# Batches 1 and 2: the next batch's first hash in one piece behind the first gate and value pair, instead of in two pieces around it

## The chip, the cores and the metric

The kernel runs on one core of one Trainium2 chip. The metric is the device time of one execution in microseconds (us); a lower one is better. A version is told by the median of several runs, and a separate execution is profiled.

## The reference

Four batches of eight heads, 768 positions and a head size of 64. Attention is masked by a hash: query and key see each other only where the signs of six projections agree. The attended heads, side by side, are the 512 wide input `x` of a gated layer with a residual.

```
q_bits = (einsum('bhsd,dk->bhsk', q, proj) > 0)        # 6 bits, the same for k
mask   = q_bucket[:, :, :, None] == k_bucket[:, :, None, :]
scores = where(mask, (q @ k.T) / sqrt(64), -1e9)
attn   = softmax(scores);  x = attn @ v                # heads side by side: 3072 x 512
h      = gelu(x @ w_gate) * (x @ w_val)                # 3072 x 1536
out    = x + sigmoid(x @ w_res) * (h @ w_out)
```

## The kernel before, in words

**The stages.** Work goes batch by batch. The attention of a batch takes 36 slots (four pairs of heads, nine chunks each): `scores` (L373) multiplies keys and queries into a PSUM tile `sp` and ScalarE takes the exponential to `e` (L385), and `values` (L345) multiplies `e` by the values into `av`, two slots later. `finish` (L299) divides on VectorE (L306, L307) and, for the batches in the middle, has SyncE issue a DMA transpose of the result `x_tok` to `x_sb` (L310), one per pair of heads. Then comes the gated layer's first half, `gate_val` (L403): for each of twelve blocks `m`, TensorE multiplies `x_sb` by `wg` into one `sp` tile (the gate) and by `wv` into the other (the value), L399, with four steps of the contraction each; one step is a matmul of 512 columns and one of 256. ScalarE takes the gelu of the gate (L416) and VectorE multiplies it by the value into `hh` (L419). There are only two `sp` tiles, so that the next block's gate waits for the gelu of this one's, and the next block's value for the product of this one's.

The layer's second half, `project` (L425), is a generator that hands out one matmul at a time: for each of six row tiles four matmuls with `wr` into `rps` (L431, ScalarE takes its tanh, L435) and twelve with `wo` into `fps` (L445), then two VectorE operations (L448, L451) and a store from SyncE (L453). The matmuls of batch b's projection are spread over the attention slots of batch b+1, some are kept (`HELD`), and `mlp_mm(NMM)` issues all that are left.

**The hash.** The raw queries and keys of a pair are transposed in blocks of 32 on VectorE (`tr`, L194, to `t32`). `hash_mm` (L197) multiplies them by the projection in float32: four operands (the two pairs' queries and keys) stand in the four column strips of the array, 32 columns each, beside one another, and write one PSUM tile `hs`. `hashed(ps, i0, i1)` (L515) issues steps i0 to i1 of four steps; a step is four matmul instructions of the program, which the profile shows as eight matmuls. So the whole hash of two pairs is x32 in the profile and half of it x16, all at L205. Then `tokens` transposes `hs` back (L215, VectorE), `bits` compares with zero and writes the bits beside the cast data in `nat` (L224, VectorE), and `turn` has SyncE issue a DMA transpose of `nat` to `aug` (L248), which the next batch's `scores` read.

**The order.** It is written out by hand: the program's order is each engine's order, and the pools only add the waits. At the end of the attention of batch 1 and of batch 2 the program issues, on TensorE: three of the four contraction steps of gate and value for m = 0 (`begun`, the last step needs the last pair's `x_sb`), what is left of the projection, the first half of the hash of the next batch's first two pairs, and then `gate_val`, which issues the last step of gate and value for m = 0 (four matmuls), calls `beside()` (the second half of the hash), and goes on with m = 1 to 11. Behind m = 0 the list `gv_work` (L585) puts `tokens` of that hash. Batch 0 and batch 3 have orders of their own, which the change leaves as they are. A second hash, of the other two pairs, stands whole behind block m = 6 (L592).

Of the kernel before, what the change touches and what calls it, by code (L numbers as in the profile page):

```python
# [17 lines left out]
def kernel(  # L18
# [178 lines left out]
    def hash_mm(jobs, dhs=(0, 1), hs_=(0, 1)):  # L197
        if jobs[0] not in hsum:
            hsum[jobs[0]] = mm_ps.tile([P, HT, 32], FP32, tag="r", name="hs")
        hs = hsum[jobs[0]]  # L200
        for hh in hs_:
            sl = slice(hh * T, hh * T + T)
            for dh in dhs:
                for j, x in enumerate(jobs):
                    nc.tensor.matmul(hs[32 * j:32 * j + 32, sl], projw[:, dh, :],  # L205
                                     t32[x][:, sl, dh, :], start=(dh == 0), stop=(dh == 1),
                                     tile_position=(0, 32 * j))
# [127 lines left out]
    def x_turn(b, hp):  # L335
        pt = mm_ps.tile([P, T, P], BF16, tag="f" if b == 0 else "r", name="pt")
        for t in range(T):
            nc.tensor.transpose(pt[:, t, :], x_tok[b][:, hp, t, :], ident)
        if hp == HP - 1:
            nc.scalar.activation(x_sb[b][:, hp, 0:2], pt[:, 0:2], AF.Copy)  # L340
            nc.vector.tensor_copy(x_sb[b][:, hp, 2:T], pt[:, 2:T])
        else:
            nc.vector.tensor_copy(x_sb[b][:, hp], pt)

    def values(p, c, e):  # L345
        va = vaug[p]
        for i in range(2):
            hi, parts = banks[2 * c + i]
            first = p < HP and (p, hi) not in av
            opened(p, hi)  # L350
            off = i * 512
            for (jt, qt0, nq) in parts:
                for qt in range(qt0, qt0 + nq):
                    nc.tensor.matmul(av[p, hi][:, qt, :], e[:, off:off + P],  # L354
                                     va[:, hi, jt, 0:D + 1],
                                     start=first, stop=(p >= HP and jt == T - 1),
                                     skip_group_check=True)
                    first = False
                    off += P
            if (2 * c + i + 1) % NCH == 0:  # L360
                if p < HP:
                    preset(p, hi)
                if (p, hi) not in late:
                    finish(p, hi)
# [4 lines left out]
    def flush():  # L369
        while pending:  # L370
            values(*pending.pop(0))

    def scores(p, c):  # L373
        qs, ks = aug[p, 0], aug[p, 1]
        sp = sc_ps.tile([P, 1024], FP32, tag="sp", name="sp")
        for i in range(2):
            hi, parts = banks[2 * c + i]
            off = i * 512
            for (jt, qt0, nq) in parts:
                nc.tensor.matmul(sp[:, off:off + nq * P], ks[0:KA, hi * T + jt, :],  # L380
                                 qs[0:KA, hi * T + qt0:hi * T + qt0 + nq, :],
                                 start=True, stop=True)
                off += nq * P
        e = e_pool.tile([P, 1024], BF16, tag="e", name="e")
        nc.scalar.activation(e, sp, AF.Exp, scale=float(ALPHA))  # L385
        return p, c, e
# [6 lines left out]
    def gv_mm(b, m, w, k0, k1, sp=None):  # L393
        xs = x_sb[b].rearrange("p k t n -> p k (t n)")
        if sp is None:
            sp = sc_ps.tile([P, 1024], FP32, tag="sp", name="sp")
        for kk in range(k0, k1):
            for c0, c1 in ((0, 512), (512, S)):
                nc.tensor.matmul(sp[:, c0:c1], w[:, kk, bass.ts(m, P)], xs[:, kk, c0:c1],  # L399
                                 start=(kk == 0), stop=(kk == KM - 1))  # L400
        return sp

    def gate_val(b, begun, beside):  # L403
        for m in range(KF):
            ps = []
            for i, w in enumerate((wg, wv)):
                if m == 0:
                    sp = gv_mm(b, m, w, KM - 1, KM, begun[i])
                else:
                    sp = gv_mm(b, m, w, 0, KM)  # L410
                ps.append(sp)
                if m == 0 and i == 1:
                    beside()
                if w is wg:
                    gt = g_pool.tile([P, S], BF16, tag="gt", name="gt")
                    nc.scalar.activation(gt, sp[:, 0:S], AF.Gelu)  # L416
            if m == 0:
                hidden[b] = hh_pool.tile([P, KF, S], BF16, tag="hh", name="hh")
            nc.vector.tensor_mul(hidden[b][:, m, :], gt, ps[1][:, 0:S])  # L419
            for piece in gv_work.pop((b, m), []):  # L420
                piece()
# [78 lines left out]
    def gv(b, m, *pieces):  # L500
        gv_work.setdefault((b, m), []).extend(pieces)
# [13 lines left out]
    def hashed(ps, i0=0, i1=4):  # L515
        jobs = [(p, side) for p in ps for side in range(2)]
        for i in range(i0, i1):
            hash_mm(jobs, (i % 2,), (i // 2,))
# [84 lines left out]
    def mlp_mm(n):  # L603
        while mlp and n > 0:
            try:
                next(mlp[0])
                n -= 1
                done[0] += 1
            except StopIteration:
                mlp.pop(0)  # L610

    for s in range(LAST):
        p, c = divmod(s, NCH)
        b, slot = divmod(s, NSLOT)
        cur = scores(p, c)
        for piece in side_pe.pop(s, []):
            piece()
        if b >= 1:
            mlp_mm(AHEAD + (slot + 1) * (NMM - HELD - AHEAD) // NSLOT - done[0])
        pending.append(cur)  # L620
        while len(pending) > LAG:
            values(*pending.pop(0))
        for piece in side_work.pop(s, []):
            piece()
        if slot == NSLOT - 1:
            values(*pending.pop(0))
            ps = (HP * (b + 1), HP * (b + 1) + 1)
            if b == 0:
                nc.scalar.activation(table, warm[:, 0:1], AF.Gelu)
                begun = [gv_mm(0, 0, wg, 0, KM - 1)]  # L630
                values(*pending.pop(0))
                begun.append(gv_mm(0, 0, wv, 0, KM - 1))
                x_turn(b, HP - 1)
                hashed(ps, 0, 3)
                gate_val(b, begun, lambda: hashed(ps, 3, 4))
            else:
                mlp_mm(4)
                flush()
                begun = [gv_mm(b, 0, w, 0, KM - 1) for w in (wg, wv)]
                if b < B - 1:  # L640
                    mlp_mm(NMM)
                    hashed(ps, 0, 2)
                    gate_val(b, begun, lambda: hashed(ps, 2, 4))
                else:
                    x_turn(b, HP - 1)
                    mlp_mm(HELD - 7)
                    gv(b, 0, lambda: mlp_mm(NMM))
                    gate_val(b, begun, lambda: mlp_mm(3))
            done[0] = 0
            mlp.append(project(b))  # L650
# [33 lines left out]
```

## Time and profile before

| | |
|---|---|
| median of three runs | 347.27 us (346.83 to 347.31) |
| profiled execution, from its first to its last instruction (span) | 345.9 us, 1.4 below that median |
| TensorE matmuls (PE) busy | 337.9 us, 98% of the span |
| VectorE (DVE), ScalarE (ACT), GpSimd (POOL) busy | 191.5, 206.9 and 86.1 us |
| granted TensorE clock, mean | 1.000 |
| hash matmuls of L205 | 3% of the chain that ended last |

Of the profiled execution no other time than its span is known; what lies around the span, the start and the end of the program, is taken as the 1.4 us between span and median. The chain that ended last is followed back from the last instruction, at each step to what released it or to the instruction before it on its engine. A piece of it gives the start and the length in us, the engine, the tile and the line, and how many instructions it holds.

### The profile page before, as it was taken

How to read it: one execution, taken by the hardware profiler on the slowest of the kernel's cores; microseconds unless marked ns; L12 is line 12 of the kernel's file. 1: busy time of each engine (PE TensorE's matmuls, PEld its weight loads, DVE VectorE, ACT ScalarE, POOL GpSimd, SP SyncE). 2: the span in 40 equal slices, each digit the busy share in tenths (PEclk: the TensorE clock that was granted, in tenths of full speed). 3: DMA queues.
4: the chain of work that ended last, by engine and by line, in shares of the span. 5: the costliest groups of instructions: out<-in, count | busy, mean ns of one | idle time of the engine just before them, and what ended most of it. 6: DMA issues, size and time to landing. Idle time of an engine off the chain costs nothing.

```text
span 345.9 us, 7597 instructions
## 1 busy us (share of the span) xinstructions
PE 337.9 (98%) x3112; PEld 204.4 (59%) x3112; DVE 191.5 (55%) x403; ACT 206.9 (60%) x232; POOL 86.1 (25%) x162
## 2 busy tenths in 40 slices
PE   8999999999999999999999999999999999999994
PEld 5667665655666655555666665655566665556442
DVE  6877757755344856757344784747244444333333
ACT  3889973226999952225999882222999984223120
POOL 4779940343055000270044100242030000000000
PEclk9999999999999999999999999999999999999999
DMA  7939999979376843518366642725430220000022
GB/s 218 377 67 239 247 265 195 159 89 223 121 178 196 195 106 78 106 34 154 85 182 190 223 117 61 136 48 105 79 100 32 55 55 30 32 1 0 32 75 78
DMA packets 71171, 42.90 MB, mean 124 GB/s; under 512 B 49504, under 2 KB 68192, under 8 KB 71136
## 3 DMA queue, kind: packets, MB, share of 16 engines
q1 hardware_dynamic: 64720, 37.17, 42.4%
q0 software_dynamic: 6336, 5.24, 10.2%
q8 instruction: 24, 0.39, 0.4%
q14 instruction: 11, 0.09, 0.1%
q10 hardware_dynamic: 80, 0.00, 0.0%
HBM read 29.36 MB, written 6.29 MB: 103 GB/s over the span
## 4 chain that ended last, share of the span: by engine, by line
PE 89%; ACT 5%; DVE 3%; issue 1%; DMA 1%; SPq 0%; DVEq 0%; ACTq 0%
PE sp L399 36%; PE fps L445 18%; PE sp L380 15%; PE av L354 8%; PE rps L431 5%; ACT e L385 4%; PE hs L205 3%; PE pt L259 2%; DMA ld<-in_q_dram 1%; DVE o L451 1%; DVE o L448 1%; DVE nat L224 0%; PE hs L234 0%; DVE ht L215 0%; DVE hh L419 0%
## 5 line engine op out<-in xcount | busy, mean ns | idle before, releaser
L385 ACT ACTIVATE e<-sp 128x1024 bf16<-128x1024 f32 x144 | 143.8, 1027 | 13.4 <-PE sp L380 7.8
L416 ACT ACTIVATE gt<-sp 128x768 bf16<-128x768 f32 x48 | 38.9, 811 | 93.0 <-PE sp L399 93.0
L380 PE MATMUL sp<-aug,aug 71*128 71x256 bf16 (+1 forms) x384 | 86.1, 325 | 1.1 <-ACT e L385 0.6
L445 PE MATMUL fps<-wo,hh 128*128 128x512 bf16 (+2 forms) x300 | 79.5, 370 | 0.0
L419 DVE TENSOR_TENSOR hh<-gt,sp 128x768 bf16<-128x768 bf16 x48 | 45.8, 955 | 50.5 <-PE sp L399 45.3
L399 PE MATMUL sp<-x_sb,wg 128*128 128x512 bf16 (+1 forms) x384 | 71.0, 326 | 0.1
L399 PE MATMUL sp<-x_sb,wv 128*128 128x512 bf16 (+1 forms) x384 | 70.9, 326 | 0.2 <-DVE hh L419 0.2
L354 PEld LDWEIGHTS <-e 128*128 128x128 bf16 x1152 | 53.3, 97 | 29.1 <-issue 1.4
L354 PE MATMUL av<-va,e 128*128 128x65 bf16 x1152 | 58.9, 193 | 0.1
L399 PEld LDWEIGHTS <-wv 128*128 128x128 bf16 x384 | 37.5, 98 | 25.1 <-issue 0.4
L399 PEld LDWEIGHTS <-wg 128*128 128x128 bf16 x384 | 36.6, 98 | 26.3 <-issue 3.0
L445 PEld LDWEIGHTS <-hh 128*128 128x128 bf16 x300 | 27.5, 97 | 22.7 <-issue 0.3
L448 DVE SCALAR_TENSOR_TENSOR o<-th,fps 128x512 f32<-128x512 f32 (+2 forms) x25 | 16.6, 666 | 36.6 <-PE fps L445 32.0
L380 PEld LDWEIGHTS <-aug 71*128 71x128 bf16 x384 | 29.4, 97 | 10.9 <-issue 2.1
L184 POOL TENSOR_SCALAR nat<-ld 128x768 bf16<-128x768 f32 (+1 forms) x16 | 14.1, 884 | 76.8 <-DMA aug<-nat 73.0
L281 POOL TENSOR_TENSOR v<-ldv 128x384 f32<-128x384 f32 x16 | 16.0, 998 | 66.7 <-DMA ldv<-in_v_dram 66.6
L194 DVE STREAM_TRANSPOSE t<-ld 128x768 f32<-128x768 f32 (+1 forms) x34 | 30.8, 913 | 1.2 <-DMA ld<-in_q_dram 1.0
L333 DVE COPY av<-av 128x390 f32<-128x390 f32 x24 | 13.6, 567 | 30.0 <-PE av L329 30.0
L431 PE MATMUL rps<-wr,x_sb 128*128 128x512 bf16 x96 | 27.1, 378 | 0.0
L435 ACT ACTIVATE th<-rps 128x512 f32<-128x512 f32 x24 | 14.3, 594 | 18.4 <-PE rps L431 18.4
L224 DVE TENSOR_SCALAR nat<-htp 32x72 bf16<-32x72 f32 x96 | 21.9, 228 | 1.8
L451 DVE SCALAR_TENSOR_TENSOR o<-o,x_tok 128x512 f32<-128x512 f32 (+2 forms) x25 | 18.2, 727 | 0.9
(61 smaller groups left out, 191.2 us busy)
## 6 DMA issues: line engine op xcount, KB each, us to landing
ldv<-in_v_dram SPq DMA_DIRECT2D x16, 384.0 KB, 5.5
out_dram<-o SPq DMA_DIRECT2D x23, 256.0 KB, 2.0
ld<-in_q_dram SPq DMA_DIRECT2D x15, 384.0 KB, 5.2
ld<-in_k_dram SPq DMA_DIRECT2D x15, 384.0 KB, 6.2
wg<-in_moe_w_gate_dram POOLq DMA_DIRECT2D x4, 384.0 KB, 8.0
wv<-in_moe_w_val_dram POOLq DMA_DIRECT2D x4, 384.0 KB, 9.8
wo<-in_moe_w_out_dram POOLq DMA_DIRECT2D x3, 512.0 KB, 6.2
wr<-in_moe_w_res_dram POOLq DMA_DIRECT2D x1, 512.0 KB, 12.8
```

Of the source, the lines that this page charges most:

```text
L194: nc.vector.transpose(t32[p, side][:, sl].rearrange("p c h n -> p (c h n)"), raw[p, side][:, sl].rearrange("p c d -> p (c d)"))
L224: engs[a % len(engs)].tensor_scalar(nat_of(x)[32 * a:32 * a + 32, :, D:D + NBITS], ht[32 * j:32 * j + 32, :, NBITS * a:NBITS * (a + 1)], 0 ...
L354: nc.tensor.matmul(av[p, hi][:, qt, :], e[:, off:off + P], va[:, hi, jt, 0:D + 1], start=first, stop=(p >= HP and jt == T - 1), skip_group ...
L380: nc.tensor.matmul(sp[:, off:off + nq * P], ks[0:KA, hi * T + jt, :], qs[0:KA, hi * T + qt0:hi * T + qt0 + nq, :], start=True, stop=True)
L385: nc.scalar.activation(e, sp, AF.Exp, scale=float(ALPHA))
L399: nc.tensor.matmul(sp[:, c0:c1], w[:, kk, bass.ts(m, P)], xs[:, kk, c0:c1], start=(kk == 0), stop=(kk == KM - 1))
L416: nc.scalar.activation(gt, sp[:, 0:S], AF.Gelu)
L419: nc.vector.tensor_mul(hidden[b][:, m, :], gt, ps[1][:, 0:S])
L431: nc.tensor.matmul(rps, x_sb[b][:, kk, t, :], wr[:, kk, :], start=(kk == 0), stop=(kk == KM - 1))
L445: nc.tensor.matmul(fps[:, cs], hh[:, m, bass.ts(t, P)], wo[:, m, cs], start=(m == 0), stop=(m == KF - 1))
L448: nc.vector.scalar_tensor_tensor(o[:, cs], th[:, cs], 1.0, fps[:, cs], op0=ALU.add, op1=ALU.mult)
L451: nc.vector.scalar_tensor_tensor(o3, o3, 0.5, x_tok[b][:, k0:k1, t, :], op0=ALU.mult, op1=ALU.add)
```

## The change

```diff
@@ -639,8 +639,7 @@
                 begun = [gv_mm(b, 0, w, 0, KM - 1) for w in (wg, wv)]
                 if b < B - 1:
                     mlp_mm(NMM)
-                    hashed(ps, 0, 2)
-                    gate_val(b, begun, lambda: hashed(ps, 2, 4))
+                    gate_val(b, begun, lambda: hashed(ps))
                 else:
                     x_turn(b, HP - 1)
                     mlp_mm(HELD - 7)
```

The branch is taken for b = 1 and b = 2. The hash's first two steps no longer stand between the rest of the projection and the last step of gate and value for m = 0; all four steps stand together behind that last step, and ahead of the gate of m = 1. No instruction is added or removed, and the order on VectorE, ScalarE, GpSimd and SyncE is the same as before.

## The prediction

> **What bounds the kernel now.** I read the page first: its busy times and its clock row.
>
> ```profile
> PE 337.9 (98%) x3112; PEld 204.4 (59%) x3112; DVE 191.5 (55%) x403; ACT 206.9 (60%) x232; POOL 86.1 (25%) x162
> ...
> PEclk9999999999999999999999999999999999999999
> ```
>
> TensorE is busy in 98% of the span, at the full granted clock in every slice, and no other engine is over 60%. In such a kernel what counts is how many nanoseconds TensorE's own stream takes, and whether a wait opens in it. Second, then, the chain that ended last, in order of time, around the place of the change in batch 1 (start us, length us, what):
>
> ```profile
> 127.65 2.59 PE fps L445 x12
> 130.24 0.79 PE hs L205 x16
> 131.03 0.76 PE sp L399 x4
> 131.78 0.79 PE hs L205 x16
> 132.57 15.71 PE sp L399 x96
> 148.28 1.44 PE hs L205 x32
> ```
>
> Here are the rest of the projection, the first half of the hash, the last contraction step of gate and value for m = 0, the second half, and then m = 1 to 6. The last row is the other hash, which stands whole. Every piece is TensorE's and each starts where the one before ends: nothing is waited for. Batch 2 shows the same lengths, from 210.73 (0.79, then 0.76, then 0.79) to 213.06. Third, what could come too late after the move: the timelines of SyncE, ScalarE and VectorE in the same stretch (start, length, engine, line, and in brackets the idle time before), and the landing time in the answer for the tile `x_sb`, from 120 to 134 us.
>
> ```profile
> 126.55 1.22 SPq L310 DMA_TRANSPOSE x_sb<-x_tok  x1
> ```
>
> ```profile
> 131.50 0.81 ACT L416 ACTIVATE gt<-sp 128x768 bf16<-128x768 f32 x1 [4.10 <-PE sp L399]
> ```
>
> ```profile
> 130.33 0.69 DVE L448 SCALAR_TENSOR_TENSOR o<-th,fps 128x512 f32<-128x512 f32 x1 [3.81 <-PE fps L445]
> 131.06 0.69 DVE L451 SCALAR_TENSOR_TENSOR o<-o,x_tok 128x512 f32<-128x512 f32 x1
> 132.34 0.95 DVE L419 TENSOR_TENSOR hh<-gt,sp 128x768 bf16<-128x768 bf16 x1 [0.59 <-ACT gt L416]
> 133.21 0.59 DVE L215 STREAM_TRANSPOSE htp<-hs 128x384 f32<-128x384 f32 x1
> ```
>
> ```profile
> DMA to landing us min/median/max: 2.7/2.7/2.7
> ```
>
> The reader is to see the release times: the last pair's `x_sb` has landed at 126.55 + 2.7 = 129.25, the gelu of m = 0 ends at 132.31, its product at 133.29.
>
> **The change part by part.** *TensorE's stream.* Nothing is added or removed; only the order differs, and with it how often TensorE goes from the whole array in bf16 to four strips in float32 and back: twice each way before, once after. The cost of that is in the rows. Two halves take 0.79 each, 1.58 together; the same 32 instructions in one piece take 1.44 (row at 148.28). That saves 0.14. The four gate and value matmuls take 0.76 between two hash halves; in the long row 96 of them take 15.71, so 0.164 each and 0.65 for four, when bf16 matmuls of the same array stand around them. Before them will then stand the projection's matmuls, also bf16 over the whole array; where these two kinds meet today the chain shows no charge (twelve of L399 from 125.70 take 1.95, 0.163 each, and twelve of L445 behind them 2.59, which ends where the next piece starts). The way into the hash stays and is inside the 1.44. So this saves 0.11. From 130.24 to the gate of m = 1 the path is now 132.57 - 130.24 = 2.33, and after 0.65 + 1.44 = 2.09: **0.24 us less, in each of two batches, 0.48 in all.** The bounds from both sides: the whole hash can't cost more here than two halves (then 0.11 per batch, 0.22 in all), unless something is waited for, which is a rival below; and no more than 0.24 can go, because all other instructions remain.
>
> *The wait for `x_sb`.* The last step of gate and value waits for the last pair's transpose. It moves from 131.03 to 130.24, and the transpose landed at 129.25: 0.99 to spare. Behind this wait stands all of TensorE. I cost it at nothing; the twelve projection matmuls (2.59) cover it. Without the cover it costs what the landing lies behind 130.24.
>
> *The wait for the gelu.* The gate of m = 1 needs the first `sp` tile. The gelu starts 131.50 - 131.03 = 0.47 after the gate's piece does and takes 0.81, so 1.28 in all. Before, 0.76 + 0.79 = 1.55 stood over it (0.27 to spare); after, 2.09 (0.81 to spare). Nothing, and safer than now.
>
> *VectorE.* Gelu is over at 130.24 + 1.28 = 131.52, but VectorE has L451 until 131.75. The product then runs from 131.75 to 132.70 and not from 132.34 to 133.29: 0.6 earlier. The value of m = 1 needs it at 132.33 + 1.31 = 133.64 (eight matmuls of 0.164 for the gate before it), so 0.9 is to spare. L215 comes next in VectorE's order and needs the whole hash, which ends at 132.33 instead of 132.57, so it starts no later than about 132.7 and not at 133.21. The four `bits` operations and the DMA transpose of L248 on SyncE follow, about half a microsecond earlier. TensorE waits for none of them in this stage: the `aug` that they make is read by the scores from about 163 on. So this is worth nothing; a later transpose would cost nothing either.
>
> *Behind this place.* From the gate of m = 1 on, all engines take their pace from TensorE. In batch 2's attention TensorE is busy for 39.82 of 40 us:
>
> ```profile
> 165.00:205.00 40.00, 39.82 (x454) 24.79 (x453) 22.56 (x44) 37.09 (x40) 9.42 (x16) 1.00 0.56 163
> ```
>
> (The first number after the length is TensorE's.) An earlier start is thus handed on almost whole. Loads are issued by slots in the program's order and move along.
>
> **Sum:** the profiled span of 345.9 becomes 345.4. What lies around it, 1.4, stays, so from the median of 347.27 comes 346.8, a gain of 0.14%. A measurement of this kernel can tell about 0.2% (0.7 us) from no change, so the likeliest verdict is no difference.
>
> **The rivals.** *First: the transpose is late, and the kernel gets slower.* Place: the first matmul of the last gate step in batches 1 and 2. Before, the first half of the hash stood ahead of this wait as work that didn't need `x_sb`. After, it stands behind. If the landing comes at a time X after 131.03, the old order ends at X + 0.76 + 0.79 and the new one at X + 0.65 + 1.44: 0.54 worse in each batch, 1.08 in both, 348.35 us. It decides from a landing of 130.24 + 0.24 = 130.48, that is 3.9 us after the issue instead of 2.7. For it: the thirteen transposes of L310 need 2.7 at least, 2.8 in the median and 6.6 at most, so longer ones occur. Against it: both that matter (126.55 and 207.04) landed after 2.7, and from 129.3 to 130.3 the DMA engines carry nothing. I give it 0.11. On this the Trainium skill speaks against the change: "DMA: Bandwidth & Descriptors", Rules for kernel authors, says to issue a DMA early and to wait on its semaphore late, with computation between. By that rule the hash belongs ahead of the wait; so far the trace says that the projection is computation enough.
>
> *Second: the gain is not handed on,* 347.27 (347.0 to 347.5). A transfer with a clock of its own would have to bound a later stage, or a new stall to take the 0.48 back. Against it are the 39.82 of 40 us; for it, that in this attention VectorE's L448 and L451 appear in the chain (178.68 and 179.40), so the cover there is thin. That the order is not changed as said belongs here; TensorE's instructions in the two programs show exactly this one move, twice. Together 0.12.
>
> *Third: more than the sum.* Near 177 and 187 VectorE's L451 takes 1.30 and 1.34 beside a busy GpSimd, against 0.69 at 131.06, and TensorE shows gaps there:
>
> ```profile
> 176.60:181.30 4.70, 4.64 (x52) 2.76 (x49) 2.56 (x4) 4.10 (x5) 3.85 (x7) 1.00 0.54 130
> 187.10:190.30 3.20, 3.09 (x32) 1.77 (x30) 2.14 (x3) 2.81 (x4) 3.04 (x7) 1.00 0.33 61
> ```
>
> Gaps of 0.06 and 0.11 could close if the stage falls differently: 0.17 in each of two later attentions, 0.34 in all, and 346.45 us. Nothing in the change moves GpSimd against VectorE there, so 0.10.
>
> **How the numbers follow.** The forecast has a chance of 0.67, at 346.8, and with the spread of the runs shown (0.48 from lowest to highest) its own range is 346.5 to 347.1. The range of 346.4 to 347.4 takes in the second and the third rival and leaves out the first, and the outer parts of the others. Faster by over 0.2% means under 346.58: most of the third rival (0.09) and the lower tail of the forecast (0.11), 0.20. Slower by over 0.2% means over 347.96: the first rival (0.11) and a stall of the second kind (0.02), 0.13. Within: 0.67.
>
> **What would show it.** In the chain after, around 130 us: L445, then four of L399 in 0.65, then 32 of L205 in 1.44, then the 96 of L399 from about 132.33, and the same again at about 210.5 with its end 0.48 earlier than now. The gelu would start near 130.71 and the product near 131.75. Wrong would be: a gap of TensorE ahead of the four matmuls, with a landing of the transpose behind 130.24 (first rival); the two places as said but the later stages no earlier (second); a hash of over 1.44 in one piece.

## The result, and the profile after

The changed kernel takes 346.74 us in the median of sixteen runs (346.31 to 347.20), the kernel before 347.27 in as many (346.83 to 347.70). The ratio is 0.9984, with an interval of 0.9978 to 0.9991: a small gain, clear of the scatter, and under the 0.2% by which the forecast separated no difference from faster. The forecast was 346.8 us and a gain of 0.48; the measured gain is 0.53.

The profiled execution has a span of 344.9 us, against 345.9. Its page shows the same picture: TensorE is busy almost throughout, at the full granted clock, and no other engine is over 60%. The program has as many matmuls as before; 48 records of them are missing from this trace, which makes the busy time smaller and leaves pieces of 0.05 called "issue" in the chain:

```profile
PE 334.2 (97%) x3064; PEld 204.3 (59%) x3112; DVE 191.4 (56%) x403; ACT 206.7 (60%) x232; POOL 86.3 (25%) x162
```

The chain that ended last, in order of time, around the place in batch 1 (start, length in us, what):

```profile
129.18 1.03 PE fps L445 x4
130.21 0.65 PE sp L399 x4
130.86 1.44 PE hs L205 x32
132.30 1.73 PE sp L399 x10
```

and in batch 2:

```profile
208.94 1.03 PE fps L445 x4
209.97 0.65 PE sp L399 x4
210.62 1.44 PE hs L205 x32
212.05 1.73 PE sp L399 x10
```

From the end of the projection to the gate of m = 1 it is 2.09 and 2.08, where 2.33 stood in both batches: the 0.65 and the 1.44 came out to the hundredth. The timelines of ScalarE and VectorE in the same stretch show who waits:

```profile
130.57 0.81 ACT L416 ACTIVATE gt<-sp 128x768 bf16<-128x768 f32 x1 [3.21 <-PE sp L399]
```

```profile
131.03 0.69 DVE L451 SCALAR_TENSOR_TENSOR o<-o,x_tok 128x512 f32<-128x512 f32 x1
131.63 0.95 DVE L419 TENSOR_TENSOR hh<-gt,sp 128x768 bf16<-128x768 bf16 x1
```

The gelu of m = 0 ends at 131.38, 0.9 ahead of the gate that needs its tile, and the product follows L451 without idle time. In front of the four L399 there is no gap: the projection's row before them ends where they start, at 130.21 and at 209.97. So the transpose, which landed at 129.28 and 209.01 (2.8 and 2.7 us after its issue), was not waited for.

The two profiles are 1.0 apart, twice the medians' distance. The starts of the gelu of m = 1 divide this: 134.01 and 214.51 before, 133.74 and 213.50 after. Batch 1's place is 0.27 earlier, of which the place itself is 0.24 and all that lies ahead of it 0.03; from one gelu to the next are 80.50 before and 79.76 after. Of those 0.74 less, 0.24 is batch 2's place. The other 0.50 arises in the attention between, where the change touches nothing; "Batch 2 alone" and "Both kernels once more" below are on that. So of the 1.0 between the two profiles only 0.48 is the change.

### The profile page after: what moved, and what is told of

Same layout as the page of the kernel before. It is cut to its first block, busy times and chain, and to the rows that moved or that the text cites. A ratio compares the mean times of both kernels' runs of the same rounds, so it can differ in the third digit from the quotient of the medians.

```text
span 344.9 us, 7549 instructions
## 1 busy us (share of the span) xinstructions
PE 334.2 (97%) x3064; PEld 204.3 (59%) x3112; DVE 191.4 (56%) x403; ACT 206.7 (60%) x232; POOL 86.3 (25%) x162
## 4 chain that ended last, share of the span: by engine, by line
PE 88%; ACT 4%; DVE 2%; DMA 2%; issue 2%; SPq 1%; POOL 0%; DVEq 0%; ACTq 0%
PE sp L399 36%; PE fps L445 18%; PE sp L380 15%; PE av L354 8%; PE rps L431 6%; ACT e L385 4%; PE hs L205 3%; DMA ld<-in_k_dram 2%; PE pt L259 1%; DVE o L451 1%; DVE nat L224 0%; SPq L96 0%; DVE o L448 0%; DVE ht L215 0%; DVE hh L419 0%
## 5 line engine op out<-in xcount | busy, mean ns | idle before, releaser
L445 PE MATMUL fps<-wo,hh 128*128 128x512 bf16 (+2 forms) x274 | 74.7, 369 | 1.6
L399 PE MATMUL sp<-x_sb,wv 128*128 128x512 bf16 (+1 forms) x379 | 70.6, 325 | 0.4 <-DVE hh L419 0.2
L399 PE MATMUL sp<-x_sb,wg 128*128 128x256 bf16 (+1 forms) x373 | 70.4, 324 | 0.7
L399 PEld LDWEIGHTS <-wv 128*128 128x128 bf16 x384 | 37.6, 98 | 25.1 <-issue 0.3
L399 PEld LDWEIGHTS <-wg 128*128 128x128 bf16 x384 | 36.8, 98 | 26.2 <-issue 2.3
L448 DVE SCALAR_TENSOR_TENSOR o<-th,fps 128x512 f32<-128x512 f32 (+2 forms) x25 | 16.6, 666 | 36.6 <-PE fps L445 31.0
L431 PE MATMUL rps<-wr,x_sb 128*128 128x512 bf16 x90 | 25.3, 378 | 0.2
L307 DVE TENSOR_TENSOR x_tok<-av,rec 128x384 bf16<-128x384 f32 x32 | 17.8, 557 | 1.1
```

The source lines that it names most:

```text
L307: nc.vector.tensor_mul(x_tok[b][:, hp, :, hi * D:(hi + 1) * D], o[:, 0:T, 0:D], rec.unsqueeze(2).to_broadcast([P, T, D]))
L431: nc.tensor.matmul(rps, x_sb[b][:, kk, t, :], wr[:, kk, :], start=(kk == 0), stop=(kk == KM - 1))
L445: nc.tensor.matmul(fps[:, cs], hh[:, m, bass.ts(t, P)], wo[:, m, cs], start=(m == 0), stop=(m == KF - 1))
L448: nc.vector.scalar_tensor_tensor(o[:, cs], th[:, cs], 1.0, fps[:, cs], op0=ALU.add, op1=ALU.mult)
```

## The experiments

The theory: TensorE's stream is the bound, and each pair of switches (whole array in bf16 to float32 strips and back) that goes saves 0.24 us. The rivals: the place of the hash counts, or something that VectorE, ScalarE or the DMA do earlier; part of the gain is scatter; and the first rival of the prediction, which the result doesn't show because its condition did not occur.

**Three pieces.**

```diff
-                    mlp_mm(NMM)
-                    hashed(ps, 0, 2)
+                    mlp_mm(6)
+                    hashed(ps, 0, 1)
+                    mlp_mm(NMM)
+                    hashed(ps, 1, 2)
                     gate_val(b, begun, lambda: hashed(ps, 2, 4))
```

> The first half of the hash is cut once more: a quarter stands in the middle of the rest of the projection, a quarter behind that, half behind the gate and value pair. Three pieces, the rest as before. Theory (a pair of switches costs about 0.24): 0.24 more in each batch, 347.75 us; the trace shows each quarter as x8 of about 0.46. Rival (the gain came from the shift of VectorE, SyncE or the gelu, not from the pieces): the projection and the pair end no later than by the hash that stands ahead of them, as before, 347.27 us.

Measured: 347.62 us, ratio 1.0010 to the kernel before (1.0001 to 1.0019), so slower by 0.35 with an interval from 0.03 to 0.66, in which the expected 0.48 lies. The chain in batch 1:

```profile
125.50 1.95 PE sp L399 x12
127.45 1.30 PE fps L445 x6
128.75 0.46 PE hs L205 x8
129.21 0.16 issue
129.37 1.24 PE fps L445 x5
130.61 0.46 PE hs L205 x8
131.07 0.76 PE sp L399 x4
131.83 0.79 PE hs L205 x16
132.62 3.03 PE sp L399 x18
```

From `begun` (the first row) to the gate of m = 1 are 7.12 us. The same stretch takes 6.87 in the kernel before (125.70 to 132.57) and 6.63 in the changed one (125.67 to 132.30). One, two and three pieces make 6.63, 6.87 and 7.12: a constant price of 0.24 to 0.25 per piece. The rival, by which only the shift of other engines counted, falls.

**The whole hash in front.**

```diff
-                    gate_val(b, begun, lambda: hashed(ps))
+                    hashed(ps)
+                    gate_val(b, begun, lambda: None)
```

> The whole hash stands ahead of the last gate and value step of m = 0 in batches 1 and 2, nothing behind it. One piece, as in the changed kernel. Theory (the place counts too: what stands behind the pair covers the 1.28 us from the start of the gate's last step to the end of its gelu): the four matmuls of 0.65 leave the gate of m = 1 waiting until about 1.3 after their start, so 1.44 + 1.3 = 2.75 instead of 2.33 before and 2.09 after: 0.42 worse than before in each batch, 348.1 us. Rival (only the number of pieces counts): as after, 346.75 us.

Measured: 348.22 us against 347.34 beside it, ratio 1.0025 (1.0014 to 1.0036). In the chain of batch 1:

```profile
130.60 1.44 PE hs L205 x32
132.04 0.44 PE sp L399 x2
...
132.51 0.82 ACT gt L416
...
133.37 1.78 PE sp L399 x10
```

A piece of ScalarE now stands in TensorE's chain: the gate of m = 1 waits for the gelu. From the hash to that gate are 2.77 us (2.75 expected, 2.33 before, 2.09 in the changed kernel). The wait for the gelu thus costs 0.68 per batch, which is more than the 0.24 of the single piece. So one piece is worth its 0.24 only where something covers the gelu's 1.3 us; that it stands behind the pair is part of the gain.

**What the switch is.** The changed kernel gets matmuls ahead of the pair whose result is overwritten: in batch 1 bf16 in strips, in batch 2 float32 over the whole array.

```diff
+                    first = (ps[0], 0)
+                    hs = hsum[first] = mm_ps.tile([P, HT, 32], FP32, tag="r", name="hs")
+                    for i in range(4):
+                        if b == 1:
+                            for j in range(4):
+                                nc.tensor.matmul(hs[32 * j:32 * j + 32, 0:T], ident[:, 0:32], wo[:, 0, 0:T * 32],
+                                                 start=True, stop=True, tile_position=(0, 32 * j))
+                        else:
+                            nc.tensor.matmul(hs[:, 0:T], projs[:, i % 2, :], t32[first][:, 0:T, i % 2, :],
+                                             start=True, stop=True)
                     gate_val(b, begun, lambda: hashed(ps))
```

> The changed kernel with matmuls added whose result is overwritten: ahead of the gate and value pair, in batch 1 sixteen bf16 matmuls of 192 columns in four strips of 32 columns each, in batch 2 four float32 matmuls of 192 columns over the whole array. One look, for the starts around them. Theory A (the switch between the whole array and strips is what costs): batch 1 shows about 0.1 us each way around its piece, batch 2 none. Theory B (the switch between bf16 and float32 is what costs): the other way round. Both may cost. With the pieces themselves (some 0.3 and 0.65) the time would be about 348.0 us.

Measured: 348.25 us in a single run. The added pieces took 0.44 and 1.30, where some 0.3 and 0.65 were expected. The chain in batch 1, then in batch 2:

```profile
129.98 0.44 PE hs L647 x16
130.42 0.76 PE sp L399 x4
```

```profile
210.28 1.30 PE hs L650 x8
211.58 0.65 PE sp L399 x4
```

The four matmuls of the pair are the gauge. Behind bf16 strips they take 0.76, as between the two hash halves before; behind float32 over the whole array 0.65, as behind bf16. That is the way out of the strips: 0.11 from strips of either type, nothing from the whole array of either type. For the way in, the starts in the timeline tell: the bf16 strips start at 129.91, 0.07 ahead of the modelled end of the projection's last matmul (129.98, where their piece of the chain begins), the float32 matmuls over the whole array at 210.12, 0.16 ahead of it (210.28). The strips come 0.09 later, and so do the float32 strips of the kernel before (130.17 against 130.24). So the change of type costs nothing, and the change between the whole array and strips costs about 0.1 us each way; the rest of the 0.24 is not resolved by these rows. The Trainium skill, "TensorEngine Tiling (Array Packing)", Key Properties, says that changing the tiling mode drains TensorE. The 0.09 and 0.11 at the change of mode agree with that; the trace shows the later starts, not the draining itself.

**Batch 2 alone.**

```diff
-                    gate_val(b, begun, lambda: hashed(ps))
+                    if b == 1:
+                        hashed(ps, 0, 2)
+                    gate_val(b, begun, lambda: hashed(ps, 2 if b == 1 else 0, 4))
```

> Only batch 2 has the hash in one piece; batch 1 keeps its two. Theory (each pair of switches between the whole array in bf16 and the float32 strips that goes saves 0.24 us, and nothing else happens): half of the gain, 347.03 us against 347.27. In the trace the path from the last L445 of the rest of the projection to the gate of m = 1 is 2.33 in batch 1 and 2.09 in batch 2, and the stage near 183 to 193 us, ahead of the one place that is changed, runs as in the kernel before. Rival (the profile pair before/after, 1.0 apart, tells that the shift in batch 1 also gains about 0.5 near 183 to 193 us in the attention behind it): a gain of 0.24 at most here, and then batch 1 alone was worth more than batch 2.

Measured: 347.25 us against 347.34, ratio 0.9995 (0.9986 to 1.0003), which takes in 0.9993 and also 1, so the time alone settles nothing. In the trace the path is 2.33 in batch 1 and 2.08 in batch 2, and from gelu to gelu are 79.76 us (134.39 to 214.15): the same as with both changed. With batch 2's 0.24 put back this stage takes 80.00, as in the changed kernel's first profile, although batch 1 has its old order here. The extra half microsecond isn't batch 1's doing.

**Both kernels once more, unchanged.**

> The kernel before once more, for a second profile. The two profiles at hand are 1.0 apart (345.9 and 344.9), the medians 0.53. Theory (the part beyond 0.48 is scatter between executions: 0.25 from the first loads, 0.5 from the attention near 183 to 193 us): this profile's span falls anywhere in 345.2 to 346.2, and the starts near 183 to 193 us against those near 134 us differ from the first profile by some tenths. Rival (the stage near 183 to 193 us is systematically shorter in the changed order): it shows the same lengths there as the first profile, to 0.1.

> The changed kernel once more, for a second profile. Theory (scatter): a span in 344.6 to 345.6, the two places at 2.09 again, and the stage from 134 to 212 us differing from the first profile of this kernel by some tenths. Rival (systematic): the stage from 134 to 212 us takes the same as in its first profile, to 0.1, and 0.5 less than in both profiles of the kernel before.

Measured: spans of 345.8 (before) and 345.9 (after), single times of 347.49 and 347.59. From gelu to gelu are 80.29 before, and 80.05 after, that is 80.29 with batch 2's 0.24 put back. So this stage took 80.50 and 80.29 in the order of before, 80.00 and 80.29 in the order of after: it scatters by half a microsecond, and the pair of first profiles lay at its two ends. The second profile of the changed kernel, whose span was expected at 344.6 to 345.6, began its attention later (the first chunks' exponentials, 0.5 later than in the first profile of before), which hid its gain of 0.48 in the span.

**The changed kernel beside others, timed again.**

> The changed kernel again, beside the others of this call on the same chip. Theory: 0.48 under the kernel before, ratio 0.9986, and in the trace 2.09 at both places. Rival (part of the 0.53 was scatter): 0.2 or less under it.

Measured: 346.98 us against 347.30, ratio 0.9986 (0.9977 to 0.9995). That is the forecast's ratio; the places have 0.65 and 1.44 again. From gelu to gelu are 79.85 (134.03 to 213.88), 80.09 with batch 2's 0.24 put back, which lies between the others.

**The cover taken away.** The first rival needs a wait for the transpose. Here the projection's twelve matmuls no longer stand ahead of the pair, once with the whole hash behind, once with half in front:

```diff
-                    mlp_mm(NMM)
-                    gate_val(b, begun, lambda: hashed(ps))
+                    gate_val(b, begun, lambda: (mlp_mm(NMM), hashed(ps)))
```

```diff
-                    mlp_mm(NMM)
-                    gate_val(b, begun, lambda: hashed(ps))
+                    hashed(ps, 0, 2)
+                    gate_val(b, begun, lambda: (mlp_mm(NMM), hashed(ps, 2, 4)))
```

> The changed kernel without the cover for the transpose: the rest of the projection (12 matmuls, 2.59 us) moves behind the gate and value pair, ahead of the whole hash. Theory (the pair waits for the landing of the transpose, which the trace of after shows at 129.28): TensorE is free for the pair at 127.62 and stands still for 1.66 us, in both batches: 346.74 + 3.3 = 350.1 us. The kernel with half of the hash left in front, sent beside it, is then 1.08 us faster, because the order in two pieces has work to do in the wait. Rival (the transpose isn't waited for until later, or the landing is not what the trace shows): the time stays at 346.7, and the other is slower by 0.5.

> The kernel before without the cover: half of the hash, the gate and value pair, the rest of the projection, the other half. Theory: the half hash fills 0.79 of the 1.66 us, TensorE stands still for 0.87 in each batch: 347.27 + 1.75 = 349.0 us, 1.08 less than with the whole hash behind. Rival as in the other run: 347.3 us, and slower than the other by 0.5.

Measured: 350.39 us (ratio 1.0084, 1.0069 to 1.0099) and 350.35 (1.0082, 1.0064 to 1.0100), four runs each. Both are some 3 us slower, but no difference between them is to be seen, where 1.08 was expected. The timelines of TensorE show the waits as expected, 1.72 with the whole hash behind (first row) and 0.91 with half in front; in the second kernel, however, there is another, in the third row:

```profile
129.12 0.49 PE L399 MATMUL sp<-x_sb,wg 128*128 128x512 bf16 x2 [1.72 <-DMA x_sb<-x_tok]
```

```profile
129.56 0.48 PE L399 MATMUL sp<-x_sb,wg 128*128 128x512 bf16 x2 [0.91 <-DMA x_sb<-x_tok]
135.38 1.47 PE L399 MATMUL sp<-x_sb,wv 128*128 128x512 bf16 x8 [0.23 <-DVE hh L419]
```

Counted from the end of the wait, the gelu of m = 1 starts 6.28 later with the whole hash behind (129.12 to 135.40) and 5.63 later with half in front (129.56 to 135.19): 0.65 per batch for the old order. One block on, at m = 2, it is 8.88 (138.00) against 8.63 (138.19), only 0.25, which four runs each don't resolve: the value of m = 1 had waited for VectorE, which had L448 and L451 of the late projection ahead of the product. The next pair moves these two behind the product (`mlp_mm(12)` in place of `mlp_mm(NMM)` in both, and the rest, `mlp_mm(NMM)`, at the head of block 0's list).

> Half of the hash, the gate and value pair, the twelve projection matmuls, the other half, as in the run without cover; but the two VectorE operations of the projection's last tile stand behind the product of m = 0. Theory (in that earlier run the half hash did fill the wait for the transpose, and the value of m = 1 then lost 0.4 per batch to VectorE, which had those two operations ahead of the product): the value of m = 1 waits for nothing, about 349.5 us, and 1.1 to 1.3 less than with the whole hash behind. Rival (what stands ahead of the wait for the transpose is worth nothing): no difference between the two.

> The pair, the twelve projection matmuls, the whole hash, with the two VectorE operations of the projection's last tile behind the product of m = 0. Theory: TensorE stands still for 1.9 in each batch until the transpose has landed, as in the earlier run without cover, and nothing else is gained or lost: 350.4 us, 1.1 to 1.3 more than with half of the hash in front. Rival: no difference between the two.

Measured: 349.93 us (ratio 1.0076, 1.0064 to 1.0089) with half in front and 350.84 (1.0099, 1.0085 to 1.0113) with the whole hash behind; the medians are 0.91 apart, where 1.1 to 1.3 were expected, and the intervals just touch. The wait with the whole hash behind is 1.70, where 1.9 was expected. In the trace with half in front the wait at m = 1 is gone, and a smaller one has come one block later (the gelu of m = 3 starts 2.87 behind that of m = 2, where the other kernel has 2.60), because VectorE now does the two operations, the `tokens` and the `bits` ahead of the product of m = 1. So what stands ahead of a wait does fill it, as the first rival says, and of its 0.65 per batch VectorE takes a part back, 0.27 at this wait; the 0.38 per batch that are left, 0.76 in all, fit the medians. In the changed kernel none of this occurs.

**Both hashes in one piece.** By the theory one more pair of switches can go. Here both hashes of the next batch stand behind block 2, and four of the projection's matmuls cover the gelu of m = 0. `t32` gets more buffers, and VectorE's work stands in other blocks. The main lines, in the program's order:

```diff
+            gv(b, 0, lambda: mlp_mm(NMM))
+            gv(b, 1, lambda y=ys[2]: tr(*y))
+            gv(b, 2, lambda y=ys[3]: tr(*y))
+            gv(b, 2, lambda p0=p0: hashed((p0, p0 + 1)), lambda p0=p0: hashed((p0 + 2, p0 + 3), tag="f"))
...
-                    mlp_mm(NMM)
-                    gate_val(b, begun, lambda: hashed(ps))
+                    mlp_mm(8)
+                    gate_val(b, begun, lambda: mlp_mm(4))
```

> In batches 1 and 2 both hashes of the next batch stand in one piece behind block m = 2 (hs in two banks), with the VectorE work in other blocks; the wait for the gelu of m = 0 is filled by four of the twelve projection matmuls instead, whose VectorE operations stand behind the product. One pair of switches per batch instead of two. Theory (a whole hash costs 1.53 on TensorE from where the next matmul could have started, two in one piece 2.83 by the groups of four, so 0.23 less than two apart): 0.47 less than the changed kernel in both batches, 346.3 us. Rival (a new wait in the crowded blocks: the transposes of nat that were spread from m = 0 on now begin at m = 3, or the landing of x_sb, which has only 0.1 to spare with eight matmuls as its cover): as the changed kernel or slower, 346.8 to 348 us.

Measured: 347.86 us, ratio 1.0015 (1.0006 to 1.0023), slower than the kernel before and, by 0.88, than the changed one beside it (346.98). The chain in batch 1 (line numbers of this kernel):

```profile
136.96 0.95 DVE hh L424
137.92 0.90 DVE t L195
...
138.86 1.49 PE hs L206 x26
140.35 1.73 PE sp L404 x10
```

The piece waits for VectorE: the last transposition to `t32` stands behind the product of m = 2 and ends at 138.82, so that the piece lasts from 136.87 to 140.35, 3.48 and not about 2.75 (an estimate: the 1.44 of one hash and eight more groups of four, which start 0.163 apart within a hash). The pair, with less cover, took 0.80 instead of 0.65: the transpose landed at 129.94, and the pair starts right behind it. Together the losses are more than the switch is worth. A place one block later, where the transposition would be done, wasn't tried; whether a second switch pair can be saved stays open.

## Why the prediction was right

*TensorE's stream.* Every term was met: 0.65 for the pair, 1.44 for the hash, 2.09 in place of 2.33 (to 0.01), in all three profiles of the changed kernel and in both batches. The upper bound was what came; the lower bound, a hash dearer in one piece, fell. The row of the other hash, which stood whole already, was the right price for the new order, since it includes the ways in and out. What the prediction named as going from bf16 to float32 strips and back is more narrowly the change between whole array and strips.

*The waits.* The one for `x_sb` had about 1 us to spare and cost nothing. The gelu has 0.9 to spare (0.81 forecast) and starts 0.14 earlier than worked out, because the prediction counted from the start of a piece of the chain. That is the modelled end of the piece before, and the pair's first matmul starts ahead of it: by 0.07 behind a hash (130.96 against 131.03), by 0.16 behind the projection (130.05 against 130.21). The product starts at 131.63 (131.75 forecast). Without anything behind the pair the gelu's wait is real, 0.68 per batch.

*Handed on.* 0.48 in the places, 0.53 and 0.32 in the medians of two comparisons, both with 0.48 inside their intervals. That the first median came within 0.06 us of the forecast's 346.8 is partly luck, since its interval for the gain goes from 0.31 to 0.76. The second rival, nothing handed on, falls with the first interval, whose upper end is 0.9991. One number of the sum was wrong without harm: around the span lie not 1.4 us but 1.7, in every execution of which both are known (346.57 and 344.9, 347.49 and 345.8). The forecast took the same value off and put it on again. But by it the profiled execution of before took about 347.6, 0.3 above its median, and that of after lay 0.17 under its own, which is where the 1.0 between the two spans comes from.

*The first rival* is a true mechanism whose condition did not occur. Its size at the next gate was 0.65 per batch, not 0.54. The 0.76 for the old pair holds the way out of the strips, and that falls into the wait: behind the landing the pair takes 0.81 in either order (129.12 to 129.93, and 129.56 to 130.37), so what is left is the half of the hash that stands behind, 1.44 - 0.79 = 0.65. And it is not the whole price, since VectorE's backlog takes part of it back.

*The third rival* (its two L451 start at 179.40 and 188.58) looked confirmed by the first profile, with 0.50 gained in the attention of batch 2. The kernel with batch 1 unchanged shows the same 80.00, and the second profiles 80.29 for either order: scatter, not a gain.

## What to carry to other kernels

When one engine is busy for 98% of the span and only the order of its instructions changes, price the new order by a row in which the same neighbours already stand side by side, and then check the release times of every wait that moves; here that gave the length of the changed place to 0.01 us, and the time within its interval. On TensorE, keep column strips together, since each further piece cost about 0.24 us here, but keep them where they cover a wait on another engine: the same piece took 0.24 per batch off behind the pair and put 0.44 on ahead of it. A distance between two single profiles is not a gain before the stage it comes from has been seen to repeat.

## What the runs showed that was not expected

That float32 next to bf16 over the whole array costs TensorE nothing at the border (0.65 for the pair either way), while bf16 strips cost as much as float32 strips. And that the scatter between executions has one visible home: in the attention of batch 2 the same VectorE operation, L451 on 128x512, takes from 0.69 to 1.37 us. Its two instances between 176 and 194 us, in the first profile of the kernel before and of the changed one, from the rows of the tile `o` (min, median, max in ns):

```profile
L451 DVE SCALAR_TENSOR_TENSOR o<-o,x_tok x2: 1305/1324/1342, 179.4 to 188.6; 128x512 f32<-128x512 f32 x2
```

```profile
L451 DVE SCALAR_TENSOR_TENSOR o<-o,x_tok x2: 692/824/957, 179.1 to 188.1; 128x512 f32<-128x512 f32 x2
```

With the two together at 2.65, 2.44, 2.21, 2.19, 1.78 and 1.65 us, in six profiles, the stage from gelu to gelu took (with batch 2's 0.24 put back where it was gained) 80.50, 80.29, 80.09, 80.29, 80.00 and 80.00: the two go together, though not strictly. In the two profiles of before and the three of after, every L451 on 128x512 that has no GpSimd instruction beside it takes 0.69, and every longer one, at most four per execution, has one beside it; two that have one take 0.69 all the same. That GpSimd is the cause was not tested by itself.
